# Block-sparse attention and an MLP on one core: half of the masks moved off TensorE, Softplus from its table throughout, other buffers for streamed weights, and a new order on all engines

## The chip, the core and the metric

The kernel runs on one core of a Trainium2 chip. A core has engines with queues of their own: TensorE (PE in the profile), VectorE (DVE), ScalarE (ACT), GpSimd (POOL) and SyncE (SP), which here issues the DMAs. Each works through its own instructions in order and waits on semaphores for the others. The metric is the device time of one execution in microseconds. Lower is better.

## The reference

All arrays are f32.

```
# attention: B=4, H=8, S=768, D=64; blocks of 32 keys, window 16
k_sum = k in blocks of 32, max;   v_sum = v in blocks of 32, mean
local  = q k^T / 8      where |i - j| < 16, else -1e9
far    = q k_sum^T / 8 + log(32)
a      = softmax over [local, far]
attn   = a [v, v_sum]                                    # 4, 8, 768, 64
# MLP on x = attn as 3072 tokens x 512
h = x w_in                                               # w_in 512 x 2048
g = h * erf(softplus(h))
out = g w_out                                            # w_out 2048 x 512
```

## The kernel before, in words

**Tokens and stages.** The 3072 tokens are cut into 6 columns of 512. Attention goes by quads: a quad is one column and one pair of heads, 24 in all (NQ). For a quad, `scores` multiplies queries by a window of 96 keys and 24 block sums (L565) into two PSUM banks pA and pB, and `softmax` follows: maxima on DVE (`red`, L596 or L600), a negation and scaling (L610, L615), exponentials on ACT (L606), reciprocal (L618) and normalisation (L622, or L625 on ACT). Then transposes (L636), a copy to SBUF (L641), the product with the values (L662), and the split of x into a high part `xh` and a low part `xl` (L678, from the fifth column part on L706 to L719).

**Masks.** For the first MQ = 8 quads the window's mask is added by TensorE: `mask` issues an L556 and an L557 for each of the two banks before the scores are accumulated on top, and `red` then reads the two banks with two L600. For the other quads DVE adds the mask (`add`, two L591, from PSUM to SBUF), and one L596 takes the maxima.

**The MLP** goes by 24 chunks k: a token column and a quarter of the 2048 hidden columns. For k < 8, `mm1` (L765) multiplies x by w_in, in three products of high and low parts; `hout` copies the result from PSUM. For k >= FAST = 8, `products` (L806) takes a form with seven products, for which weight sums are prepared by `add_up` (L394, L397, L403, L406), written to DRAM and fetched again by `get_sums` (L433). The activation comes next. For k < SOFT = 4 it is Tanh (L781) and a Ln (L879), for the other chunks Softplus from its table (L783, L872), then Erf (L884) in both. `gsplit` multiplies by h (L896; L891 for k < 2) and splits the product into `gh` (a cast, L277) and `gl` (a subtraction, L903). `mm2` multiplies these by w_out (L920; L916 for k < 2 in plain f32).

**Weights.** `load_w` brings a 1 MB unit of w_in or w_out as 64-bit numbers. `convert` makes f32 of it on DVE (L330, L333, L336), and `split` makes a high half on ACT (`high`, a cast, L277) and a low half on DVE (`low`, L352). Conversions of 16 units stand among the first four chunks. Units of w_in stay in SBUF. The halves of w_out are written to DRAM by `put` (L366) and come back by `get` (L376, `w<-dr` in the profile) from chunk 7 on into five slots which `turn` hands out in the order of ROUND. `get_sums` takes slots from the same round. Slot 11 is also the buffer `sums` of `add_up`, whose last reader is the L406 of the last set of sums.

**Order.** Nothing is issued as it stands in the loop. `on`, `act`, `pe` and `dma` record every step in a `Plan` with its cost on each engine that may run it; `order` then lists the steps, each engine taking what is ready and has the smallest key (due time plus the step's entry in TUNE; an entry can also pin an engine). Where a step names two engines, the one that would end it first gets it. The issued program has a fixed order on each engine. FILL puts small matmuls on a tile of zeros (`busy`, L959) ahead of certain TensorE steps in the first part.

Of the kernel before, what the change touches and what calls it, by code (L numbers as in the profile page):

```python
# [23 lines left out]
NP = H // 2  # L24
# [10 lines left out]
NG = F // (128 * G)  # L35
NPER = NCH * NG
MQ = 2 * NP
# [4 lines left out]
SOFT = 4  # L42
FAST = 8
# [3 lines left out]
FILL = {20: 7, 40: 8, 41: 9, 61: 6, 93: 14, 111: 6}  # L47
# [3 lines left out]
def f32(ap):  # L51
    return ap.bitcast(F32)
# [134 lines left out]
def block_attention_mlp(ctx: ExitStack, tc: tile.TileContext, q_t, k_nat, k_win, v_tok, v_nat, v_win, w_in, w_out, out):  # L187
# [8 lines left out]
    def sb(shape, dtype, name, tag=None):  # L196

        n = math.prod(shape[1:])
        if n % 128 == 0:
            return pool.tile(shape, dtype, name=name, tag=tag or name)  # L200
        t = pool.tile([128, -(-n // 128) * 128], dtype, name=name, tag=tag or name)[0:shape[0], 0:n]
        return t if len(shape) == 2 else t.rearrange("p (a b) -> p a b", a=shape[1]) if len(shape) == 3 else t.rearrange("p (a b c) -> p a b c", a=shape[1], b=shape[2])
# [47 lines left out]
    def stat(n, par):  # L250
        return stats[:, (3 * par + n) * NB:(3 * par + n + 1) * NB]
# [12 lines left out]
    def pe(us, fn, r=(), w=(), **kw):  # L264
        return P.add({"PE": us}, lambda e: fn(), r, w, **kw)

    def on(us, fn, r=(), w=(), **kw):
        return P.add(us, lambda e: fn(engines[e]), r, w, **kw)

    def act(us, fn, r=(), w=(), **kw):  # L270
        return P.add({"ACT": us}, lambda e: fn(), r, w, **kw)
# [4 lines left out]
    def copy(e, o, i):  # L276
        e.copy(o, i) if e is nc.scalar else e.tensor_copy(o, i)  # L277

    units = [(kind, g, r) for kind, g in UNITS for r in range(2)]
    tiles, raws, whl, w32, wide = {}, {}, {}, {}, {}
    WHOLE = {0: 11, 1: 10}
    FIRST = {4: 9, 5: 8, 6: 12, 7: 13}
    LATER = {0: 12, 1: 13, 2: 9, 3: 8, 4: 9, 5: 8}
    ROUND = (12, 13, 11, 9, 8)
    ON_DVE = (0, 2)
    SUMS, TURN, RAW_X = 11, (12, 13), 10  # L290
    kept = {}

    def slot(n, shape, dtype, name):
        return sb(shape, dtype, name, f"w{n}")

    def number(u):
        return 2 * u[1] + u[2]

    def raw_slot(u):
        return number(u) if u[0] == "i" else 12 + u[2]  # L300

    def frees(n):
# [12 lines left out]

    def convert(u):

        w, s, m = f"w{raw_slot(u)}", {}, number(u)
        at_once = u[0] == "i" or u[1] >= NN
        home = f"gl{u[2]}" if at_once else f"a{m}"  # L320

        def a():
            if at_once:
                s["t"] = sb([128, 2, 512], F32, "a32", home)
            else:
                if u[2] == 0:
                    wide[u[1]] = slot(WHOLE[u[1]], [128, 2, 2, 512], F32, "a32s")
                s["t"] = w32[u] = wide[u[1]][:, u[2]]
            s["a"], s["rw"] = s["t"].bitcast(U32), raws.pop(u)
            nc.vector.tensor_scalar(s["a"], s["rw"][..., 1], 3, 0x3FFFFFFF, op0=ALU.logical_shift_left, op1=ALU.bitwise_and)  # L330

        def b():
            nc.vector.scalar_tensor_tensor(s["a"], s["rw"][..., 0], 29, s["a"], op0=ALU.logical_shift_right, op1=ALU.bitwise_or)  # L333

        def c():
            nc.vector.scalar_tensor_tensor(s["a"], s["rw"][..., 1], 0xC0000000, s["a"], op0=ALU.bitwise_and, op1=ALU.bitwise_or)  # L336

        on({"DVE": 0.6}, lambda e: a(), [w], [home] if at_once or u[2] else frees(WHOLE[u[1]]))
        on({"DVE": 1.13}, lambda e: b(), [w, home], [home])
        on({"DVE": 1.13}, lambda e: c(), [w, home], [home])  # L340
        if at_once:
            split(u, m if u[0] == "i" else FIRST[m], home, lambda: s["t"])

    def split(u, n, home, whole):
        def high(e):
            t = slot(n, [128, 2, 2, 512], F32R, "w")
            whl[u] = t[:, 0], t[:, 1]
            kept[u] = t
            copy(e, whl[u][0], whole())

        def low(e):
            e.tensor_tensor(whl[u][1], whole(), f32(whl[u][0]), op=ALU.subtract)  # L352
        on({"ACT": 0.94}, high, [home], frees(n))
        on({"DVE": 1.13}, low, [home, f"w{n}"], [f"w{n}"])

    def parts(m, n):
        u = ("o", m // 2, m % 2)
        split(u, n, f"a{m}", lambda: w32[u])
# [65 lines left out]
    def turn():  # L424
        turns[0] += 1
        return ROUND[(turns[0] - 1) % len(ROUND)]

# [117 lines left out]
    def scores(qd, banks=PA):  # L545
# [3 lines left out]
        def mask():  # L549
# [3 lines left out]
            m0 = mask_at[qd // NP % 3]  # L553
            for sc in s["sc"] if qd < MQ else []:

# [3 lines left out]
        def keys(parts):  # L559
            for j in range(NB):  # L560
                for a in range(2):
                    r, o = slice(64 * a, 64 * a + 64), slice(64 * (j % 2), 64 * (j % 2) + 64)
                    for n, rhs in parts(r, j):
                        n += j // 2 * NK
                        nc.tensor.matmul(s["sc"][a][o, n:n + rhs.shape[-1]], lhsT=s["qb"][r, 64 * j:64 * j + 64], rhs=rhs, start=qd >= MQ, stop=True, skip_group_check=True)  # L565

# [8 lines left out]
        if qd >= NP:  # L575
            pe(1.06 if qd >= MQ else 1.64, both, ["qb", "kw"] + (["mh"] if qd < MQ else []), banks)
        else:
# [4 lines left out]
    def softmax(qd, banks=PA):  # L582
# [10 lines left out]
        def red(e):  # L593
            s["mx"] = stat(0, par)
            if qd >= MQ:
                e.tensor_reduce(s["mx"], s["pr"], op=ALU.max, axis=AX.X)  # L596
# [5 lines left out]
        def exps():  # L602
            sm = s["sm"] = stat(1, par)
            for j in range(NB):
                i = j % NI
                nc.scalar.activation(s["pr"][:, j], s["pr"][:, j] if qd >= MQ else s["sc"][j // NI][:, i * NK:(i + 1) * NK], AF.Exp, scale=0.125, bias=s["mx"][:, j:j + 1], accum_out=sm[:, j:j + 1])  # L606

# [3 lines left out]

        if qd >= MQ:
            on({"DVE": 1.2}, add, banks, [pr])
# [156 lines left out]
    def hout(k, f, eng):  # L770
# [7 lines left out]
        def tanh():  # L778
            wt[k, s] = sb([128, 2, T], F32, "wt", f"wt{s}")
            if k < SOFT:  # L780
                nc.scalar.activation(wt[k, s], hc[k, s], AF.Tanh, scale=0.5)  # L781
# [6 lines left out]
    def soft(k, s, fn):  # L788
        act(0.96 if k < SOFT else 1.06, fn, [f"hc{s}"], [f"wt{s}"], table=("sig", "exp") if k < SOFT else ("soft",))

# [84 lines left out]
    def logs(k):  # L875

        for n in range(2 if k < SOFT else 0):
            s = f"wt{n}"
            act(1.06, lambda n=n: nc.scalar.activation(wt[k, n], wt[k, n], AF.Ln, scale=-0.49999994, bias=half_b), [s], [s], table=("log",))  # L879

    def erfs(k, after):
        for n in range(2):
            s = f"wt{n}"
            act(0.96, lambda n=n: nc.scalar.activation(wt[k, n], wt[k, n], AF.Erf, scale=-1.0 if k < SOFT else 1.0), [s], [s], table=("sig",), after=after)  # L884

# [135 lines left out]
    def follow(n, bank=None):  # L1021
        sums(n, bank)
        load_quad(n)
        with_quad(load_nat, n + 1)

    with_quad(load_nat, NP)
    for u in units[4:6]:
        load_w(u)

    todo = {0: units[2:6], 1: units[6:10], 2: units[10:14], 3: units[14:16]}  # L1030
    loads = {0: units[6:12], 1: units[12:14], 2: units[14:16]}
    early = FAST
    early_att = {(1, 1): [(lambda n: follow(n, "o2"), 4)], (1, 3): [(attend, 4), (follow, 5)],
                 (2, 1): [(output, 4), (attend, 5), (follow, 6)], (2, 3): [(output, 5), (attend, 6), (follow, 7)],
                 (3, 1): [(output, 6), (attend, 7), (follow, 8)], (3, 3): [(output, 7), (attend, 8), (follow, 9)]}

    for k in range(NPER):
        qa, qs = k + NP, k + NP + 1
        ch, g = divmod(k, NG)
        mult = sub = {"DVE": 1.136}  # L1040
        cast = {"DVE": 0.605, "ACT": 0.95} if NG <= k < FAST else {"DVE": 0.605}
        xeng, heng = ({"DVE": 0.6, "ACT": 0.48},) * 2 if k < early else ({"DVE": 0.6},) * 2
        for u in todo.get(k, []):
            convert(u)
        for u in loads.get(k, []):
            load_w(u)
        if k == 3:
            for m in (4, 5, 6, 7):
                put(m, FIRST[m])
        if k == 4:  # L1050
            for m in (2, 3):
                parts(m, LATER[m])
            for c in range(2):
# [95 lines left out]
    k = NPER - 1  # L1149
# [59 lines left out]
```

## Time and profile before

| | before |
|---|---|
| median of 3 runs | 629.37 us (629.01 to 630.21) |
| profiled execution | 629.01 us, span 627.2 us |
| granted clock of TensorE, mean | 0.997 |
| busy: PE, DVE, ACT, POOL | 618.2, 440.3, 409.6, 46.4 us |

The span runs from the first to the last instruction; 1.8 us of the time lie around it. The profiled execution is the fastest of the three, 0.36 us under the median. A busy time counts an engine's instructions from start to end, and neighbours overlap by some hundredths of a microsecond, so a pitch is a little less than a mean duration. In the views below, "a<-b" stands for the output and inputs by the program's names, "x4" for a count, and the engine behind "<-" ended the wait that is named.

### The profile page before, as it was taken

How to read it: one execution, taken by the hardware profiler on the slowest of the kernel's cores; microseconds unless marked ns; L12 is line 12 of the kernel's file. 1: busy time of each engine (PE TensorE's matmuls, PEld its weight loads, DVE VectorE, ACT ScalarE, POOL GpSimd, SP SyncE). 2: the span in 40 equal slices, each digit the busy share in tenths (PEclk: the TensorE clock that was granted, in tenths of full speed). 3: DMA queues.
4: the chain of work that ended last, by engine and by line, in shares of the span. 5: the costliest groups of instructions: out<-in, count | busy, mean ns of one | idle time of the engine just before them, and what ended most of it. 6: DMA issues, size and time to landing. Idle time of an engine off the chain costs nothing.

```text
span 627.2 us, 12062 instructions
## 1 busy us (share of the span) xinstructions
PE 618.2 (99%) x4840; PEld 520.9 (83%) x4840; DVE 440.3 (70%) x634; ACT 409.6 (65%) x820; POOL 46.4 (7%) x72
## 2 busy tenths in 40 slices
PE   9999999999999997999999999999999999999997
PEld 6786567888888886889899899898898898899886
DVE  5999999848799797768668657658656576425442
ACT  5669977979969677464585675565766555552550
POOL 2010000100420800000000000000000000000000
PEclk9999999999999999999999999999999999999999
DMA  8998957653585888888767776766687555574622
GB/s 327 274 364 300 330 162 254 242 193 87 186 326 178 313 286 327 286 315 285 277 222 248 267 275 215 249 222 227 221 291 253 195 181 195 202 258 157 253 72 67
DMA packets 36843, 150.23 MB, mean 240 GB/s; under 512 B 3956, under 2 KB 9396, under 8 KB 24244
## 3 DMA queue, kind: packets, MB, share of 16 engines
q1 hardware_dynamic: 36212, 148.95, 68.4%
q8 instruction: 38, 0.62, 0.4%
q10 hardware_dynamic: 576, 0.52, 0.3%
q14 instruction: 17, 0.14, 0.1%
HBM read 124.13 MB, written 23.07 MB: 235 GB/s over the span
## 4 chain that ended last, share of the span: by engine, by line
PE 91%; DVE 5%; DMA 1%; ACT 1%; issue 1%; SPq 0%; DVEq 0%
PE ops L920 37%; PE hb L806 14%; PE h L765 13%; PE ha L806 10%; PE ops L916 4%; PE px L662 4%; PE pA L565 3%; PE pA L636 2%; PE pB L636 1%; DMA w<-dr 1%; PE idle L959 1%; ACT prf L606 1%; DVE ws L406 1%; DVE gl L903 1%; DVE sums L397 0%
## 5 line engine op out<-in xcount | busy, mean ns | idle before, releaser
L920 PE MATMUL ops<-w,gh 128*128 128x512 f32 x704 | 230.1, 396 | 2.7 <-DMA w<-dr 2.7
L920 PEld LDWEIGHTS ops<-w,gh 128*128 128x128 f32 x704 | 133.0, 189 | 30.5 <-DMA w<-dr 2.9
L920 PE MATMUL ops<-w,gl 128*128 128x512 f32 x352 | 137.8, 391 | 0.0
L896 DVE TENSOR_TENSOR hc<-wt,hc 128x1024 f32<-128x1024 f32 x44 | 54.7, 1253 | 77.3 <-ACT wt L884 77.3
L1167 ACT ACT_TABLE_LOAD x83 | 106.5, 1283 | 1.5
L765 PE MATMUL h<-xh,w 128*128 128x512 f32 x256 | 86.9, 403 | 0.1
L277 ACT COPY hc<-hb 128x256 f32<-128x256 f32 x49 | 18.1, 373 | 95.4 <-DVE hc L859 40.4
L920 PEld LDWEIGHTS ops<-w,gl 128*128 128x128 f32 x352 | 66.5, 189 | 12.4
L765 PEld LDWEIGHTS h<-xh,w 128*128 128x128 f32 x256 | 48.1, 188 | 12.1 <-issue 1.1
L806 PE MATMUL hb<-w,ws 128*128 128x256 f32 x384 | 56.8, 283 | 0.0
L903 DVE TENSOR_TENSOR gl<-hc,gh 128x1024 fp32r<-128x1024 f32 x44 | 54.8, 1246 | 0.8
L606 ACT ACTIVATE pr<-pr,stats 128x120 f32<-128x120 f32 x128 | 48.8, 382 | 5.8 <-DVE stats L615 5.7
L806 PEld LDWEIGHTS hb<-w,ws 128*128 128x128 f32 x384 | 50.7, 192 | 0.2 <-DVE ws L406 0.2
L884 ACT ACTIVATE wt<-wt 128x1024 f32<-128x1024 f32 x48 | 50.6, 1062 | 0.4
L765 PE MATMUL h<-xl,w 128*128 128x512 f32 x128 | 49.9, 390 | 0.0
L527 POOL COPY kw<-ksum 128x96 f32<-128x96 f32 (+1 forms) x28 | 17.3, 632 | 405.6 <-DMA kw<-k_win 367.6
L277 DVE CAST gh<-hc 128x1024 fp32r<-128x1024 f32 x43 | 30.0, 698 | 18.1 <-PE ops L920 16.9
L872 ACT ACTIVATE wt<-hc 128x1024 f32<-128x1024 f32 x32 | 32.1, 1050 | 0.2
L277 DVE COPY hc<-hb 128x256 f32<-128x256 f32 x47 | 19.8, 422 | 15.2 <-PE hb L806 13.9
L916 PE MATMUL ops<-a32s,gw 128*128 128x512 f32 x64 | 29.3, 596 | 0.0
L806 PE MATMUL ha<-w,ws 128*128 128x256 f32 x192 | 28.5, 283 | 0.8 <-DVE w L743 0.8
L856 DVE TENSOR_TENSOR hc<-hb,hc 128x256 f32<-128x256 f32 x32 | 13.5, 422 | 22.3 <-PE hb L806 20.7
(168 smaller groups left out, 1110.7 us busy)
## 6 DMA issues: line engine op xcount, KB each, us to landing
w<-dr SPq DMA_DIRECT2D x36, 1024.0 KB
ws<-ds SPq DMA_DIRECT2D x30, 1024.0 KB
kw<-k_win SPq DMA_DIRECT2D x20, 480.0 KB
rw<-w_in SPq DMA_DIRECT2D x8, 1024.0 KB
rw<-w_out SPq DMA_DIRECT2D x8, 1024.0 KB
dr<-w SPq DMA_DIRECT2D x8, 1024.0 KB
ds<-ws SPq DMA_DIRECT2D x8, 1024.0 KB
vw<-v_win SPq DMA_DIRECT2D x20, 384.0 KB
```

The lines of the kernel that those rows point to most:

```text
L277: e.copy(o, i) if e is nc.scalar else e.tensor_copy(o, i)
L606: nc.scalar.activation(s["pr"][:, j], s["pr"][:, j] if qd >= MQ else s["sc"][j // NI][:, i * NK:(i + 1) * NK], AF.Exp, scale=0.125, bias=s ...
L662: nc.tensor.matmul(xo[r, o], lhsT=s["vw"][:, j, r], rhs=s["pt"][:, a, o], start=True, stop=True)
L765: nc.tensor.matmul(hs[k, f][:, 0:T], lhsT=w[m], rhs=xt[ch, cc][x], start=(cc == 0 and n == 0), stop=(cc == 3 and n == 2))
L806: nc.tensor.matmul(shape, lhsT=w[m], rhs=y[l], start=first and c == 0 and i == 0, stop=c == 1 and i == 2, skip_group_check=True)
L872: nc.scalar.activation(wt[k, n], hc[k, n], AF.Softplus)
L884: act(0.96, lambda n=n: nc.scalar.activation(wt[k, n], wt[k, n], AF.Erf, scale=-1.0 if k < SOFT else 1.0), [s], [s], table=("sig",), after ...
L896: e.tensor_tensor(hc[k, n], wt.pop((k, n)), hc[k, n], op=ALU.mult)
L903: e.tensor_tensor(gs[k, n][1], hc.pop((k, n)), f32(gs[k, n][0]), op=ALU.subtract)
L916: nc.tensor.matmul(os_[ch, t], lhsT=x[0][:, i % 2, t * 128:(t + 1) * 128], rhs=w32["o", g, i // 2][:, i % 2], start=first, stop=last)
L920: nc.tensor.matmul(os_[ch, t], lhsT=x[y][:, i % 2, t * 128:(t + 1) * 128], rhs=w[m], start=first and n == 0, stop=last and n == 2)
L1167: nc.scalar.preload_act_table_set(sets[o["load"]])
```

## The change

- MQ goes from 8 to 4: quads 4 to 7 get their mask from DVE as the later ones do.
- SOFT goes from 4 to 0: Softplus from its table (L783) in all chunks; Tanh and Ln go, and Erf no longer has a scale of -1.
- ROUND goes from (12, 13, 11, 9, 8) to (12, 13, 9, 8, 11).
- `low` of `split` may also run on POOL, at a planner cost of 2.9 against 1.13 on DVE; `high` of `gsplit` may run on ACT in all of the first eight chunks.
- TUNE has 2071 entries instead of 464, and other values; FILL has 30 matmuls in four places instead of 50 in six. So the order on every engine is another one.

```diff
-MQ = 2 * NP
+MQ = NP
...
-SOFT = 4
+SOFT = 0
...
-TUNE = {0: (-833.887, 1.5, 0, None), 1: (-504.34, 1.5, 0, None), ...}
-FILL = {20: 7, 40: 8, 41: 9, 61: 6, 93: 14, 111: 6}
+TUNE = {0: (-1842.48, 1.5, 0, None), ...}
+FILL = {48: 4, 51: 6, 81: 10, 86: 10}
...
-    ROUND = (12, 13, 11, 9, 8)
+    ROUND = (12, 13, 9, 8, 11)
...
         on({"ACT": 0.94}, high, [home], frees(n))
-        on({"DVE": 1.13}, low, [home, f"w{n}"], [f"w{n}"])
+        on({"DVE": 1.13, "POOL": 2.9}, low, [home, f"w{n}"], [f"w{n}"])
...
-        cast = {"DVE": 0.605, "ACT": 0.95} if NG <= k < FAST else {"DVE": 0.605}
+        cast = {"DVE": 0.605, "ACT": 0.95} if k < FAST else {"DVE": 0.605}
```

In counts of instructions: L556 and L557 on PE 16 to 8 each, L959 64 to 44; L352 on DVE 16 to 6 and on POOL 0 to 10; L591 on DVE 32 to 40, L596 16 to 20, L600 16 to 8; on ACT L781 and L879 8 to 0 each, L783 8 to 16, L625 8 to 0 with L622 on DVE 23 to 24, casts of 1024 columns 17 to 22 (on DVE 43 to 38), table loads 83 to 86 ahead of L1167.

The first place is POOL's queue from the constants to the sums. A kw copy (L527) puts block sums into a tile of keys. Before:

```order
L507 COPY vwf<-vsum 24x1024
L527 COPY kw<-ksum 128x4x24 x8
L527 COPY kw<-ksum 128x8x24 x3
L394 TENSOR_TENSOR sums<-w 128x2x256 x4
L397 TENSOR_TENSOR sums<-sums 128x2x256 x3
```

After, at the same place (a_512 and the like are the f32 units that `convert` made):

```order
L507 COPY vwf<-vsum 24x1024
L352 TENSOR_TENSOR w<-a_512,w 128x1024
L352 TENSOR_TENSOR w<-a_573,w 128x1024
L527 COPY kw<-ksum 128x4x24 x4
L352 TENSOR_TENSOR w<-a_785,w 128x1024
L352 TENSOR_TENSOR w<-a_817,w 128x1024
L352 TENSOR_TENSOR w<-a_890,w 128x1024
L527 COPY kw<-ksum 128x4x24
L352 TENSOR_TENSOR w<-a_910,w 128x1024
L527 COPY kw<-ksum 128x4x24
L352 TENSOR_TENSOR w<-a_1017,w 128x1024
L527 COPY kw<-ksum 128x4x24
```

Low halves stand between the copies now, and the copies behind them wait their turn; three more follow after these rows.

The second place is DVE's queue up to the first `gl` (L903), which the first L920 needs. Before:

```order
L277 CAST gh<-hc 128x1024
L330 TENSOR_SCALAR a_1111<-rw 128x1024
L333 SCALAR_TENSOR_TENSOR a_1111<-rw,a_1111 128x1024
L352 TENSOR_TENSOR w<-a_1073,w 128x1024
L336 SCALAR_TENSOR_TENSOR a_1111<-rw,a_1111 128x1024
L678 TENSOR_TENSOR xl<-px,xh 128x512
L600 TENSOR_REDUCE stats<-pA 128x4
L600 TENSOR_REDUCE stats<-pB 128x4
L352 TENSOR_TENSOR w<-a_1111,w 128x1024
L615 TENSOR_SCALAR stats<-stats 128x8
L330 TENSOR_SCALAR a_1197<-rw 128x1024
L903 TENSOR_TENSOR gl<-hc,gh 128x1024
```

After:

```order
L330 TENSOR_SCALAR a_1115<-rw 128x1024
L333 SCALAR_TENSOR_TENSOR a_1115<-rw,a_1115 128x1024
L610 TENSOR_SCALAR stats<-stats 128x8
L336 SCALAR_TENSOR_TENSOR a_1115<-rw,a_1115 128x1024
L618 RECIPROCAL stats<-stats 128x8
L622 TENSOR_TENSOR pr<-pr,stats 128x960
L277 CAST xh<-px 128x512
L678 TENSOR_TENSOR xl<-px,xh 128x512
L352 TENSOR_TENSOR w<-a_1115,w 128x1024
L330 TENSOR_SCALAR a_1190<-rw 128x1024
L903 TENSOR_TENSOR gl<-hc,gh 128x1024
```

From the start of the program to this first L903, DVE has 3 L352 instead of 11. It has 6 L591, 3 L596 and 2 L600 instead of 8 L600, two more L622, one L610 and one L618 more, one cast of `gh` fewer, and one cast of `xh` and one copy of `hc` more.

The third place is SP's queue around chunk 8, where the halves of w_out (dr4 to dr7) are fetched for chunks 6 and 7. Numbers are those of tiles: w_2530 and w_2339 are the tiles for dr6. Before:

```order
L376 DMA w_2190<-dr4_1182 128x2048
L410 DMA ds20_2209<-ws_2088 128x2048
L410 DMA ds21_2237<-ws_2110 128x2048
L376 DMA w_2263<-dr5_1253 128x2048
...
L376 DMA w_2422<-dr7_1398 128x2048
L536 DMA vw_2449<-v_win 96x1024
L518 DMA qb_2469<-q_t 128x512
L433 DMA ws_2482<-ds10_2007 128x2048
L540 DMA vw_2449<-vsum_109 24x8x128
L410 DMA ds00_2504<-ws_2432 128x2048
L376 DMA w_2530<-dr6_1297 128x2048
```

After:

```order
L376 DMA w_2169<-dr4_1202 128x2048
L536 DMA vw_2192<-v_win 96x1024
L518 DMA qb_2207<-q_t 128x512
L376 DMA w_2223<-dr5_1276 128x2048
L540 DMA vw_2192<-vsum_109 24x8x128
L410 DMA ds31_2246<-ws_2190 128x2048
L410 DMA ds30_2271<-ws_2197 128x2048
L376 DMA w_2339<-dr6_1326 128x2048
L410 DMA ds01_2364<-ws_2298 128x2048
L536 DMA vw_2401<-v_win 96x1024
L518 DMA qb_2427<-q_t 128x512
L376 DMA w_2434<-dr7_1367 128x2048
```

The tile for dr6 now comes ahead of that for dr7, ahead of the sums' last writes (L410 of ds0) and ahead of the first fetch of sums (L433); by ROUND it lies in slot 9, where w_2169 was, and no longer in slot 11.

2 lines of the change are left out of this document (1 added, 1 removed).

## The prediction

> **What bounds the kernel now.** I read first the page's busy time and its chain.
>
> ```profile
> PE 618.2 (99%) x4840; PEld 520.9 (83%) x4840; DVE 440.3 (70%) x634; ACT 409.6 (65%) x820; POOL 46.4 (7%) x72
> ...
> PE 91%; DVE 5%; DMA 1%; ACT 1%; issue 1%; SPq 0%; DVEq 0%
> ```
>
> TensorE (PE) is busy 618.2 of 627.2 us. A gain is therefore PE work taken away or one of its few waits taken away; a loss is a new wait. The list of PE's waits names the waits:
>
> ```profile
> PE ops L920 <- DMA w<-dr: 2.7, 1, 2.7
> PE idle L959 <- DVE zeros L212: 1.1, 1, 1.1
> PE ha L806 <- DVE w L743: 0.8, 1, 0.8
> ```
>
> The table by stages shows how near VectorE (DVE) is to being the bound in the first sixth (columns: length, then busy time of PE, PEld, DVE, ACT, POOL, PE's granted clock, DMA share and rate):
>
> ```profile
> 40.00:60.00 20.00, 20.00 (x125) 13.22 (x122) 19.61 (x24) 17.20 (x33) 0.95 (x2) 1.00 0.90 334
> 60.00:80.00 20.00, 20.00 (x102) 12.28 (x101) 19.93 (x23) 19.82 (x25) 0.00 (x0) 1.00 0.89 320
> 80.00:100.00 20.00, 20.00 (x99) 12.48 (x98) 19.33 (x23) 14.29 (x29) 1.56 (x2) 1.00 0.49 143
> ...
> 120.00:140.00 20.00, 20.00 (x147) 16.40 (x148) 9.84 (x16) 15.97 (x30) 0.69 (x2) 1.00 0.66 223
> ...
> 200.00:250.00 50.00, 46.25 (x298) 39.22 (x297) 41.92 (x56) 37.41 (x70) 15.08 (x9) 0.99 0.86 300
> ```
>
> From 40 to 100 us DVE is busy 58.9 of 60 us, and PE never waits: the two run abreast. After 120 us DVE has half its time free. The meeting point is the first `gl` (L903), which the first L920 matmul needs:
>
> ```profile
> 106.94 1.22 DVE L903 TENSOR_TENSOR gl<-hc,gh 128x1024 fp32r<-128x1024 f32 x1
> ...
> 110.47 0.16 DVE L610 TENSOR_SCALAR stats<-stats 128x8 f32<-128x8 f32 x1
> ...
> 108.54 0.39 PE L765 MATMUL h<-xh,w 128*128 128x512 f32 x1
> 108.76 0.39 PE L920 MATMUL ops<-w,gh 128*128 128x512 f32 x1
> ```
>
> DVE ends it at 108.16, and PE is there at 108.76: 0.6 us of slack. The other weak place is chunk 8, where the 200 to 250 us row has PE idle for 3.75 us. The chain of waits there:
>
> ```profile
> 237.67 1.15 DVE ws L406
> ...
> 238.87 8.58 DMA w<-dr
> ...
> 247.50 4.30 PE ops L920 x12
> ```
>
> The w_out half of get(6) comes into slot 11, the buffer of the sums, which the last L406 frees at 238.82; then it needs 8.58 us. The wait is followed by a half clock:
>
> ```profile
> 249.00:252.40 3.40, 3.40 (x11) 2.69 (x10) 1.23 (x1) 1.86 (x2) 0.00 (x0) 0.50 0.53 193
> ```
>
> 3.4 us at 0.50 cost 1.7 us.
>
> **The change, part by part.** All against the profiled run, 629.0 us (span 627.2 and 1.8 around it); it is the fastest of three, and the median is 0.4 above.
>
> Mask. PE's part of it for one quad, four matmuls ahead of the scores:
>
> ```profile
> 102.31 0.37 PE L556 MATMUL pA<-mask_h,small 128*128 128x480 bf16 x1
> ...
> 102.89 0.31 PE L565 MATMUL pA<-kw,qb 64*64 64x120 f32 x1
> ```
>
> 102.31 to 102.89 is 0.58 us. Four quads lose it: -2.3 us of PE work, all of it after the point where DVE binds, because the order puts as much other PE work ahead of the first L920 as it takes away. On DVE each such quad gets two L591 and an L596 for two L600; three of the four stand ahead of the first `gl` and are counted below, the fourth lies in DVE's free half after 120 us.
>
> ROUND. get(6) now goes to slot 9, get(7) to slot 8, and neither waits for the sums. The 3.75 us idle in that row (2.7 and 0.8 of them listed) and the 1.7 us of half clock go: -5.5 us. What is late next is get(6) itself: between the last reader of slot 9 and its first L920 stand some 6.3 us of PE work (24 matmuls of 512 columns at 0.22 to 0.23 us, the pitch of the PE rows at 108.54 and 108.76, and about 0.9 us of small ones). A landing of 8.58 us would leave 2.3 us of wait, one faster than 6.3 us none. I take none and keep 2.3 for the range.
>
> Softplus, casts and table loads, on ScalarE (ACT). In four chunks L783 takes the place of L781 and L879 goes; eight L625 go; up to five L277 casts and three table loads come:
>
> ```profile
> L1167 ACT ACT_TABLE_LOAD x83 | 106.5, 1283 | 1.5
> ...
> L277 ACT CAST w<-a 128x1024 fp32r<-128x1024 f32 x12 | 12.6, 1052 | 4.6 <-DVE a L336 4.6
> ...
> L879 ACT ACTIVATE wt<-wt,stats 128x1024 f32<-128x1024 f32 x8 | 9.3, 1160 | 0.1
> ...
> L625 ACT ACTIVATE prf<-prf,stats 128x120 f32<-128x120 f32 x8 | 2.4, 384 | 0.0
> ```
>
> -9.3 - 2.4 + 5 x 1.05 + 3 x 1.28 = -2.6 us of ACT, beside PE's work: costed at nothing. ACT is full only in the 60 to 80 us row (19.82 of 20). Were a cast put just there, the DVE operation behind it would come up to 1.05 us later; at the first `gl`, where ACT has had 14.29 of 20 us just before, that is covered.
>
> Fillers. 20 fewer L959. At the start PE waits for DVE's conversions anyway, so what goes as filler partly returns as wait:
>
> ```profile
> L959 PE MATMUL idle<-zeros 128*128 128x256 bf16 x64 | 9.7, 305 | 1.1 <-DVE zeros L212 1.1
> ```
>
> By its busy time 20 of 64 are 3.0 us: 0 to -3.0, taken -0.8, nearer to none since DVE is ahead of PE by only 0.6 us at the place where they end up. It counts only if PE, and not DVE, sets the time at the first `gl`.
>
> L352. Eight of the ten that go to GpSimd (POOL) leave DVE ahead of the first `gl`. The rows for what leaves and comes there (line, shapes, count, busy, mean ns):
>
> ```profile
> L352 DVE TENSOR_TENSOR w<-a,w 128x1024 fp32r<-128x1024 f32 x12 | 14.6, 1220 | 0.5 <-ACT w L277 0.5
> ...
> L596 DVE TENSOR_REDUCE stats<-pr 128x8 f32<-128x960 f32 x16 | 18.3, 1143 | 0.0
> ...
> L591 DVE TENSOR_TENSOR pr<-pA,mask_sb 128x480 f32<-128x480 f32 x16 | 10.4, 652 | 7.4 <-PE pB L565 7.4
> ...
> L600 DVE TENSOR_REDUCE stats<-pA 128x4 f32<-128x480 f32 x5 | 3.3, 655 | 1.1 <-PE pB L565 1.1
> ...
> L622 DVE TENSOR_TENSOR prf<-prf,stats 128x960 f32<-128x960 f32 x3 | 3.5, 1150 | 0.0
> ```
>
> Rows overlap by 0.08 us, so the pitch is that much less. By pitch: -8 x 1.14 (L352), +3 x 1.06 (L596), L591 for L600 even (6 x 0.57 each), +2 x 1.07 (L622, a quad's normalisation that now stands earlier), two 512-wide copies and casts for one 1024-wide (+0.6), 0.3 of small operations: -2.9 us. Uncontended, the first `gl` would end at 108.16 - 2.9 = 105.3, with PE there at about 108.0: 2.7 us of slack.
>
> But POOL isn't free of DVE. The one place of this trace where POOL does such work on full tiles, and DVE beside it:
>
> ```profile
> 202.71 7.33 POOL L394 TENSOR_TENSOR sums<-w 128x512 f32<-128x512 f32 x4 [2.97 <-DVE ws L406]
> 210.01 7.24 POOL L397 TENSOR_TENSOR sums<-sums 128x512 f32<-128x512 f32 x4
> ```
>
> ```profile
> 202.49 1.22 DVE L896 TENSOR_TENSOR hc<-wt,hc 128x1024 f32<-128x1024 f32 x1
> 203.62 2.32 DVE L903 TENSOR_TENSOR gl<-hc,gh 128x1024 fp32r<-128x1024 f32 x1
> 205.86 0.94 DVE L452 TENSOR_REDUCE vs_sum<-rows 128x24 f32<-128x768 f32 x1
> ...
> 207.88 1.01 DVE L277 CAST gh<-hc 128x1024 fp32r<-128x1024 f32 x1 [0.23 <-PE ops L920]
> 208.82 1.25 DVE L610 TENSOR_SCALAR stats<-stats 128x8 f32<-128x8 f32 x1
> ...
> 211.35 2.02 DVE L622 TENSOR_TENSOR pr<-pr,stats 128x960 f32<-128x960 f32 x1
> ```
>
> ```profile
> 175.47 1.29 POOL L397 TENSOR_TENSOR sums<-sums 128x512 f32<-128x512 f32 x1
> ```
>
> Alone a POOL operation on 512 columns takes 1.29 us; here 1.83. Beside it the L903 takes 2.32 instead of 1.22, and the L610, a few columns, 1.25 instead of the 0.16 at 110.47, while the reduce L452 keeps its 0.94. That is not a shared rate: one waits until the other's whole instruction is over, and operations that read one tile to a few numbers, or read PSUM, are spared. An L352 on POOL is twice as long, 2 x 1.29 = 2.6 us. From below: from 203.6 to 213.4 DVE lost 3.4 us (1.1 in L903, 0.3 in the cast, 1.1 in L610, 0.9 in L622 against its 1.15) to 5.3 POOL operations, 6.8 us of POOL's own work: 0.5 us for each us of POOL, 1.3 for an L352. From above: every L352 blocks one for nearly its length, 2.3. I take 1.8, the middle, because most DVE work in that stage (conversions, L891, L903) is of the kind that blocks, and a reduce of 0.94 no longer covers 2.6. 8 x 1.8 = 14.4: the first `gl` ends at 119.7 instead of 108.16, and PE, 0.1 later, starts at 119.8 instead of 108.76: +11.0 us. Queued behind it on PE is everything after, and DVE has room only later. After such a wait I count one half-clock period, +1.7.
>
> [...]
>
> Sum: 629.0 + 11.0 + 1.7 - 2.3 - 5.5 = 633.9, say 634.
>
> **Rivals.**
> 1. POOL's part hides, DVE isn't held: no wait at the first `gl`. 629.0 - 2.3 - 5.5 - 0.8 = 620.4. For it: the conversions leave DVE 2.9 us less nominal work. Against: the 2.32 us row. It decides at a loss of 2.7 / 8 = 0.34 us for each L352; below that this is the case. It is the one that ends faster.
> 2. DVE is held, but at the low end, 1.3: the first `gl` at 115.7, +7.0, and 629.0 + 7.0 + 1.7 - 2.3 - 5.5 = 629.9; without the half clock 628.2. No difference to be measured, or little.
> 3. DVE is held to the full, 2.3: the first `gl` at 123.7, +15.0: 637.9, and with the late get(6) (2.3, and 1.7 for another half clock) 641.9.
> 4. ROUND doesn't do what it says: get(6) waits as long as before in its new place. With rival 1, 620.4 + 4.0 = 624.4; with the forecast 638.
> Loss at the other weak point, POOL's queue: an L352 that stands behind a kw copy (L527) waiting for its load comes late for PE. The copies' load wait isn't in PE's list now, and this adds to case 3 rather than making one.
>
> **How the numbers follow.** Forecast (held, 1.5 to 2.1 us each, 631 to 636): 0.4. Rival 3 with the late get(6) and rival 4 on the forecast: 0.2. Rival 2: 0.13, half of it (0.07) within 0.2% (1.3 us, about what a measurement of this kernel can tell from no change), 0.02 faster, 0.04 slower. Rival 1, with rival 4 or not: 0.27. Faster 0.29, same 0.07, slower 0.64. The range must reach rival 1 at 620, since it holds more than 2 in 10, and up to the full hold: 619.5 to 641. The forecast alone: 631 to 636.
>
> **What would show it.** In the profile after: POOL's L352 with a mean over 2.6 us; DVE's conversions (L333, L336) beside them at 2 to 3.5 us instead of 1.22; in PE's list waits for `gl` or `gw` (L903, L891) or `w` of some 11 us before 130 us, with a clock of 0.5 behind; no wait of L920 on the load around chunk 8 over 2.3 us; four L556 pairs fewer. If PE waits for DVE under 1 us in all and the span is near 619, rival 1 held. If the mean of L333 and L336 stays at 1.22 and PE is still late, my mechanism is wrong whatever the time.

## The result, and the profile after

The changed kernel takes 636.81 us (median of four runs, 635.39 to 638.65) against 629.19 before: 1.0128 times as long, with a 95% interval of 1.0089 to 1.0167. The forecast was 634 with a range of 619.5 to 641, on the slow side. The profiled execution is the slowest of the four, 638.65 us with a span of 636.9, 9.7 more than before.

Busy times and chain of the page, after:

```profile
PE 618.1 (97%) x4804; PEld 517.6 (81%) x4804; DVE 442.0 (69%) x621; ACT 411.2 (65%) x815; POOL 82.4 (13%) x82
...
PE 81%; DVE 11%; ACT 3%; DMA 2%; issue 1%; SPq 1%; ACTq 0%
```

PE's busy time is 0.1 us from that of before, with less work in it: slices at half clock are a part of what makes it longer (two stretches of 3.4 us at 0.50, at 27 and at 98 us, where before had one). The span grew, so the loss is waiting. PE's waits, after:

```profile
PE ops L916 <- DVE gw L891: 3.1, 2, 1.7
PE ops L916 <- DVE a32s L336: 3.1, 1, 3.1
PE h L565 <- issue: 1.6, 1, 1.6
PE pA L636 <- DVE pr L622: 1.3, 1, 1.3
PE px L662 <- DMA vwf<-v_win: 1.3, 1, 1.3
PE h L765 <- DVE hc L277: 1.3, 1, 1.3
```

The wait on `w<-dr` is gone, and most of what has come ends at DVE. The stages (same columns as in the prediction):

```profile
14.00:40.00 26.00, 23.13 (x320) 17.71 (x320) 21.75 (x32) 15.43 (x58) 3.50 (x2) 0.93 1.01 268
40.00:60.00 20.00, 17.14 (x120) 11.92 (x120) 19.25 (x19) 13.32 (x15) 5.23 (x4) 1.00 0.74 273
60.00:80.00 20.00, 18.32 (x90) 10.61 (x89) 19.83 (x21) 17.28 (x33) 6.35 (x4) 1.00 0.95 324
80.00:100.00 20.00, 16.92 (x85) 10.44 (x84) 20.00 (x22) 12.82 (x28) 9.41 (x5) 0.96 0.49 159
...
200.00:250.00 50.00, 48.69 (x333) 39.30 (x332) 45.56 (x60) 38.70 (x57) 14.53 (x9) 1.00 0.66 236
```

Where PE lost nothing from 40 to 100 us before, it is now idle 7.6 of 60 us, with DVE busy 59.1. At 200 to 250 it is idle 1.3 instead of 3.75. The meeting point, on DVE and on PE:

```profile
122.07 1.22 DVE L903 TENSOR_TENSOR gl<-hc,gh 128x1024 fp32r<-128x1024 f32 x1
```

```profile
123.50 0.39 PE L920 MATMUL ops<-w,gh 128*128 128x512 f32 x1
```

The first L920 starts at 123.50 instead of 108.76, 14.7 later; from there to the end it is 513.4 instead of 518.4 us, 5.0 less.

### The profile page after: what moved, and what is told of

It is laid out like the page before. It is cut to its first block, busy times and chain, and to the rows that moved or that the text cites. A ratio compares the mean times of both kernels' runs of the same rounds, so it can differ in the third digit from the quotient of the medians.

```text
span 636.9 us, 11998 instructions
## 1 busy us (share of the span) xinstructions
PE 618.1 (97%) x4804; PEld 517.6 (81%) x4804; DVE 442.0 (69%) x621; ACT 411.2 (65%) x815; POOL 82.4 (13%) x82
## 4 chain that ended last, share of the span: by engine, by line
PE 81%; DVE 11%; ACT 3%; DMA 2%; issue 1%; SPq 1%; ACTq 0%
PE ops L920 38%; PE hb L806 14%; PE ha L806 11%; PE h L765 8%; PE px L662 3%; DMA vwf<-v_win 2%; PE pA L565 2%; DVE a L333 2%; DVE a L336 2%; PE pA L636 2%; PE pB L636 2%; ACT L1167 1%; DVE a L330 1%; DVE pr L622 1%; DVE hc L896 1%
## 5 line engine op out<-in xcount | busy, mean ns | idle before, releaser
L920 PE MATMUL ops<-w,gh 128*128 128x512 f32 x704 | 233.7, 396 | 0.0
L920 PEld LDWEIGHTS ops<-w,gh 128*128 128x128 f32 x704 | 132.5, 188 | 28.4 <-issue 0.9
L920 PE MATMUL ops<-w,gl 128*128 128x512 f32 x352 | 137.4, 390 | 0.0
L765 PE MATMUL h<-xh,w 128*128 128x512 f32 x256 | 91.2, 410 | 2.3 <-DVE hc L277 1.3
L920 PEld LDWEIGHTS ops<-w,gl 128*128 128x128 f32 x352 | 66.3, 188 | 12.0
L606 ACT ACTIVATE pr<-pr,stats 128x120 f32<-128x120 f32 x160 | 61.0, 382 | 8.1 <-DVE stats L615 7.9
L527 POOL COPY kw<-ksum 128x96 f32<-128x96 f32 (+1 forms) x28 | 24.0, 868 | 313.1 <-DMA kw<-k_win 297.0
L765 PEld LDWEIGHTS h<-xh,w 128*128 128x128 f32 x256 | 48.1, 188 | 15.8 <-issue 2.3
L903 DVE TENSOR_TENSOR gl<-hc,gh 128x1024 fp32r<-128x1024 f32 x44 | 56.3, 1282 | 0.8
L765 PE MATMUL h<-xl,w 128*128 128x512 f32 x128 | 50.1, 391 | 0.5 <-DVE xl L678 0.5
L277 DVE CAST gh<-hc 128x1024 fp32r<-128x1024 f32 x38 | 27.1, 713 | 15.6 <-PE ops L920 14.4
L916 PE MATMUL ops<-a32s,gw 128*128 128x512 f32 x64 | 30.7, 611 | 6.2 <-DVE gw L891 3.1
L606 ACT ACTIVATION_READ_ACCUMULATOR pr<-pr,stats 128x1 f32 x160 | 29.9, 187 | 0.0
L765 PEld LDWEIGHTS h<-xl,w 128*128 128x128 f32 x128 | 24.1, 188 | 7.0 <-issue 1.9
```

The lines of the kernel that those rows point to most:

```text
L765: nc.tensor.matmul(hs[k, f][:, 0:T], lhsT=w[m], rhs=xt[ch, cc][x], start=(cc == 0 and n == 0), stop=(cc == 3 and n == 2))
L903: e.tensor_tensor(gs[k, n][1], hc.pop((k, n)), f32(gs[k, n][0]), op=ALU.subtract)
L916: nc.tensor.matmul(os_[ch, t], lhsT=x[0][:, i % 2, t * 128:(t + 1) * 128], rhs=w32["o", g, i // 2][:, i % 2], start=first, stop=last)
L920: nc.tensor.matmul(os_[ch, t], lhsT=x[y][:, i % 2, t * 128:(t + 1) * 128], rhs=w[m], start=first and n == 0, stop=last and n == 2)
```

## The experiments

Ratios are to runs of the kernel before taken beside each kernel (their medians lie between 627.8 and 629.2), with 95% intervals. "First L920" is its start in the profiled execution.

| kernel | median us | ratio | first L920 | span |
|---|---|---|---|---|
| before | 629.2 | 1 | 108.8 | 627.2 |
| changed | 636.8 | 1.0128 (1.0089 to 1.0167) | 123.5 | 636.9 |
| e1, changed, L352 on DVE | 630.6 | 1.0026 (1.0008 to 1.0044) | 114.0 | 627.3 |
| e2, changed, POOL's L352 a memset | 623.7 | 0.9934 (0.9909 to 0.9959) | 108.5 | 621.9 |
| e3, before, L352 on POOL | 633.0 | 1.0083 (1.0054 to 1.0112) | 115.1 | 631.2 |
| e4, before, new ROUND | 625.1 | 0.9947 (0.9927 to 0.9967) | 108.4 | 622.2 |
| e5, changed again | 635.4 | 1.0124 (1.0099 to 1.0148) | 121.2 | 634.6 |
| e6, before, masks, new plan | 643.0 | 1.0254 (1.0220 to 1.0289) | 117.3 | 639.3 |
| e7, before, Softplus, new plan | 631.0 | 1.0063 (1.0039 to 1.0086) | 113.0 | 631.5 |
| e8, changed, POOL's L352 in quarters | 629.9 | 1.0029 (1.0015 to 1.0043) | 115.4 | 629.1 |
| e9, before, masks, order kept | 631.5 | 1.0052 (1.0026 to 1.0079) | 109.5 | 627.7 |
| e10, before, Softplus, order kept | 630.5 | 1.0051 (1.0030 to 1.0072) | 111.6 | 627.9 |
| e11, before, ROUND and quarters | 626.9 | 0.9984 (0.9967 to 1.0001) | 109.6 | 623.4 |
| e12, e11 with fewer fillers | 627.0 | 0.9981 (0.9963 to 1.0000) | 111.0 | 624.8 |

**Is it GpSimd that holds VectorE?** First the changed kernel with the low halves back on DVE.

```diff
+        if "low" in o:
+            o["on"] = "DVE"
         o["fn"](o["on"])
```

> The changed kernel with all ten L352 of GpSimd back on VectorE, at the same places of the order. Theory (GpSimd's L352 hold VectorE): VectorE loses the 13 us of stretched operations before the first gl and gets 8 x 1.14 = 9.1 us of work back, so the first L920 comes 3 to 4 us earlier than its 123.5, about 633 us. Rival (the L352 on GpSimd are hidden and the order alone is late): VectorE gets 9 us more and loses none, 645 us. L333 and L336 return to a mean of 1.22 to 1.28 us under the theory.

630.6 us, 6 less than the changed kernel. DVE has 9.1 us more to do ahead of the first L920 and reaches it 9.5 us earlier than in the first trace (7.2 earlier than in e5's), more than the 3 to 4 expected. The stretches at half clock are gone, too: the mean clock is 1.000. PE still waits 3.5 us for L891 and L336 there, against 6.2 in the changed kernel, so a part of these waits belongs to the rest of the change. DVE's groups with what stretched, first of the changed kernel from 14 to 130 us, then of e1 from 14 to 123 us:

```profile
L333 DVE SCALAR_TENSOR_TENSOR a<-rw,a 128x1024 uint32<-128x1024 uint32 x12 | 18.9, 1578 | 0.1
L336 DVE SCALAR_TENSOR_TENSOR a<-rw,a 128x1024 uint32<-128x1024 uint32 x12 | 16.3, 1362 | 0.1
...
L891 DVE TENSOR_TENSOR gw<-wt,hc 128x1024 f32<-128x1024 f32 x4 | 7.0, 1758 | 0.6 <-ACT wt L884 0.6
L336 DVE SCALAR_TENSOR_TENSOR a32s<-rw,a32s 128x1024 uint32<-128x1024 uint32 x4 | 6.9, 1732 | 0.0
L622 DVE TENSOR_TENSOR pr<-pr,stats 128x960 f32<-128x960 f32 x3 | 5.5, 1825 | 0.0
...
L596 DVE TENSOR_REDUCE stats<-pr 128x8 f32<-128x960 f32 x4 | 4.6, 1148 | 0.0
```

```profile
L336 DVE SCALAR_TENSOR_TENSOR a<-rw,a 128x1024 uint32<-128x1024 uint32 x12 | 14.6, 1218 | 0.1
L333 DVE SCALAR_TENSOR_TENSOR a<-rw,a 128x1024 uint32<-128x1024 uint32 x12 | 14.6, 1218 | 0.1
...
L336 DVE SCALAR_TENSOR_TENSOR a32s<-rw,a32s 128x1024 uint32<-128x1024 uint32 x4 | 4.9, 1224 | 0.0
...
L891 DVE TENSOR_TENSOR gw<-wt,hc 128x1024 f32<-128x1024 f32 x4 | 4.9, 1220 | 0.6 <-ACT wt L884 0.6
...
L622 DVE TENSOR_TENSOR pr<-pr,stats 128x960 f32<-128x960 f32 x3 | 3.5, 1153 | 0.0
```

Count times the difference of the means: 4.3 + 1.7 + 2.2 + 2.0 + 2.0 = 12.2 us in these groups. The reduce L596 did not stretch (1.148 us, 1.144 in e1), but none of the four lies beside an L352 on POOL. Others do: from 74.88 to 81.63 us POOL has two L352, and beside them the reduce L452 keeps its 0.94 us (0.943 in e1) and the two L591, which read PSUM and SBUF, their 0.64 (0.648 and 0.646), where the L891 takes 3.36 instead of 1.22:

```profile
76.06 3.36 DVE L891 TENSOR_TENSOR gw<-wt,hc 128x1024 f32<-128x1024 f32 x1
79.33 0.94 DVE L452 TENSOR_REDUCE vs_sum<-rows 128x24 f32<-128x768 f32 x1
80.20 0.64 DVE L591 TENSOR_TENSOR pr<-pA,mask_sb 128x480 f32<-128x480 f32 x1
80.76 0.64 DVE L591 TENSOR_TENSOR pr<-pB,mask_sb 128x480 f32<-128x480 f32 x1
```

All of DVE's operations together are its busy time ahead of the first `gl`, in the changed kernel, in its second trace (e5) and in e1 (length, busy time and count, then PE's clock, DMA share and rate):

```profile
0.00:122.07 122.07, 107.24 (x125) 0.97 0.79 259
0.00:119.75 119.75, 108.09 (x125) 0.99 0.78 264
0.00:112.55 112.55, 102.19 (x133) 1.00 0.83 278
```

Without its eight L352 (9.1 us) e1 would have 93.1. So DVE lost 14.1 and 15.0 us, 1.8 to 1.9 for each of the eight L352. Not only operations with two inputs in SBUF were held: L330 reads one tile, takes 0.69 us in the mean in e1, and once, in e5, beside an L352 on POOL from 34.21 to 36.60 us, took 2.90:

```profile
34.24 2.90 DVE L330 TENSOR_SCALAR a<-rw 128x1024 uint32<-128x1024 uint32 x1
```

One case by itself, on POOL and on DVE, from the timelines of the changed kernel:

```profile
37.87 2.49 POOL L352 TENSOR_TENSOR w<-a,w 128x1024 fp32r<-128x1024 f32 x1 [18.97 <-ACT w L277]
```

```profile
38.15 3.30 DVE L333 SCALAR_TENSOR_TENSOR a<-rw,a 128x1024 uint32<-128x1024 uint32 x1
```

L352 ends at 40.36; the L333 ends at 41.45, 1.1 later, about its own length (1.22 in e1). The next pair repeats it: an L352 from 44.60 to 47.00 us, and an L333 of 3.41 from 44.68, which ends 1.1 behind it. By these two rows it moved when the other was over. The next experiment leaves the engine and the time and takes the reading away.

```diff
-            e.tensor_tensor(whl[u][1], whole(), f32(whl[u][0]), op=ALU.subtract)
+            e.memset(f32(whl[u][1]), 0.0) if e is nc.gpsimd else e.tensor_tensor(...)
```

> The changed kernel, but the ten low halves that GpSimd makes are filled with zeros by a memset of the same 128x1024 tile, which reads nothing (the low parts of those weights are left out). Theory (VectorE is held while GpSimd reads two tiles of SBUF): L333, L336, L891, L622 return to 1.15 to 1.3 us, the first L920 comes 9 to 12 us earlier, 625 us, with one or two half-clock periods fewer. Rival (GpSimd holds VectorE by writing too): still some 1 us for each, 631. Rival (the order or the loads at the start are late whatever GpSimd does): 636.

623.7 us. POOL's L352, and DVE's L333 beside it:

```profile
L352 POOL MEMSET w<- 128x1024 f32 x10 | 9.5, 960 | 35.2 <-DVE a L336 28.3 <-issue 6.9
```

```profile
L333 DVE SCALAR_TENSOR_TENSOR a<-rw,a 128x1024 uint32<-128x1024 uint32 x12 | 14.7, 1223 | 0.1
```

Beside GpSimd's memset, which only writes SBUF, L333 loses nothing measurable (1.223 us, 1.218 in e1), and the first L920 is back at 108.5 us. DVE's busy time ahead of the first `gl`, for the same 125 instructions as in the changed kernel, is 13.2 us less than in its first trace and 14.0 less than in e5:

```profile
0.00:106.63 106.63, 94.06 (x125) 1.00 0.85 288
```

(The memset is also shorter, 0.96 us, and doesn't wait for the cast: what is shown by it alone is that the order isn't late of itself once DVE has this room.) With the subtraction on GpSimd the mean of L333 is 1.58 us, with the memset 1.22. Whether the missing read or the shorter instruction does it, this run alone doesn't show; the quarters of e8 below, shorter still at 0.72 to 0.75 us, read SBUF and bring L333 to 1.31.

Then the reverse, in the kernel before.

```diff
+        if o.get("low") in (('i', 0, 1), ('i', 1, 0), ..., ('o', 0, 0)):   # the same ten units
+            o["on"] = "POOL"
         o["fn"](o["on"])
```

> The kernel before with the same ten L352 (by weight unit) on GpSimd, at their places in its own order, nothing else changed. Theory: 8 of them ahead of the first gl cost VectorE 1.65 us each and free it of 1.14 each, +4 us, and the next conversions wait for the slower low halves: 633 to 637 us. Rival (GpSimd's part is hidden): VectorE gets 9 us of room, 628 to 629 us.

633.0 us, with the first L920 at 115.1, 6.4 later than before. Of this, 2.1 us lie ahead of the first L765 (31.22 instead of 29.14): PE waited 2.0 us for a load of q at 7.95 us, ahead of any L352, and ran at half clock for 3.4 us after it. The 4.3 behind the first L765 are the theory's 4. So this part alone, in an order that had nothing to do with it, costs 0.83% (0.54 to 1.12). All three runs lie at or within 2.5 us of the theory's numbers, and not at the rivals' 645, 631 and 628.

**Does the length of one hold matter?**

```diff
+            for c, h in ((0, 0), (0, 1), (1, 0), (1, 1)) if e is nc.gpsimd else ():
+                i = slice(256 * h, 256 * h + 256)
+                e.tensor_tensor(whl[u][1][:, c, i], whole()[:, c, i], f32(whl[u][0])[:, c, i], op=ALU.subtract)
+            if e is nc.gpsimd:
+                return
```

> The changed kernel with each L352 of GpSimd cut into four of 256 columns. Theory (VectorE is held for the length of one GpSimd instruction, and operations that are spared cover a part): a hold of 0.65 us is covered more often, the loss per low half falls from 1.65 towards 1.3 us, 8 x 0.35 = 2.8 us, 634 us. Rival (what counts is GpSimd's total reading time): 636 to 637 us, as whole. Rival (each piece waits for VectorE anew, and low halves come later): over 638 us.

629.9 us, 4 us better than expected. The groups on POOL (L354 is the subtraction in this kernel) and on DVE from 14 to 123 us:

```profile
L354 POOL TENSOR_TENSOR w<-a,w 128x256 fp32r<-128x256 f32 x32 | 38.3, 1227 | 36.3 <-ACT w L277 36.3
```

```profile
L333 DVE SCALAR_TENSOR_TENSOR a<-rw,a 128x1024 uint32<-128x1024 uint32 x12 | 15.7, 1312 | 0.1
```

DVE's busy time ahead of the first `gl` in this kernel:

```profile
0.00:114.53 114.53, 99.91 (x125) 1.00 0.83 274
```

A quarter takes 1.23 us in the mean, and 0.72 to 0.75 in half of the 40 cases: now POOL waits, too. DVE loses 0.09 us on an L333 instead of 0.36, and over all its operations 5.9 us against e2 (6.8 against e1 without its L352) instead of 13.2 to 15.0. Expected were 1.3 us for each low half; it is 0.7 to 0.9. The same columns are read in both kernels; what differs is the length of one instruction, at least 2.39 us for an L352 in the changed kernel's first trace. It still isn't better than L352 on DVE (e1, 1.0026 against 1.0029): DVE waited 2.4 us for loads and 1.9 us for POOL's halves.

**The start.** The first profile begins badly, so the changed kernel was profiled once more, unchanged.

> The changed kernel once more, for a second trace of its start. In its first profile the first L765 starts at 31.15 us after a late v_win load and two half-clock slices; with the same order up to there it starts at 27.3 and 28.0 in the two runs with GpSimd's L352 taken away. Theory (the late start of the first profile is a matter of that execution's loads): first L765 at 27 to 29 us, the waits of the stage with L352 as before, 635 to 637 us. Rival (GpSimd's work is what makes the start late): again 31 us.

635.4 us, and the first L765 starts at 27.5. In the first profile these slices are the difference:

```profile
27.00:28.00 1.00, 1.00 (x7) 0.50 1.27 228
28.00:29.00 1.00, 1.00 (x6) 0.50 0.86 227
29.00:30.00 1.00, 1.00 (x6) 0.50 1.04 325
```

They follow the 1.6 us wait of L565 and the late v_win load in the list above, of which e5 has 0.8 and 0.3 us. So about 2 us of the first trace's 14.7 belong to that execution and not to the change; in e5 the first L920 stands at 121.2, 12.4 us later than before, with its waits on L891 and L336 at 3.1 and 3.0 as in the first.

**ROUND alone.**

```diff
-    ROUND = (12, 13, 11, 9, 8)
+    ROUND = (12, 13, 9, 8, 11)
```

> The kernel before with the new ROUND alone. Theory: get(6) no longer waits for the sums; the wait of 2.7 us, the 0.8 of L743 as far as it hangs on it, and 1.7 us of half clock go: 624 to 626 us. Rival (the wait only moves, or get(6) is as late in slot 9): 629.

625.1 us. PE's waits in this kernel, all of them:

```profile
PE idle L959 <- DVE zeros L212: 1.1, 1, 1.1
PE hb L806 <- ACT hc L277: 0.9, 1, 0.9
PE o L565 <- issue: 0.6, 1, 0.6
PE pA L636 <- DVE pr L622: 0.4, 1, 0.4
```

The wait on `w<-dr` and the half clock behind it are gone, the span is 5.0 us shorter than in the profile of before, and a wait of 0.9 us stands in their place. The medians differ by less, 3.3 us (2.1 to 4.6); e9 below shows a reason. It is the fastest kernel of this study that computes everything, 0.53% (0.33 to 0.73) faster than before.

**Masks alone.** The first try changed the cost and the dependences that the planner sees, too.

```diff
-            for sc in s["sc"] if qd < MQ else []:
+            for sc in s["sc"] if qd < NP else []:
...
+            if NP <= qd < MQ:
+                add(e)
+                e.tensor_reduce(s["mx"], s["pr"], op=ALU.max, axis=AX.X)
+                return
...
-        on({"DVE": 1.06 if qd >= MQ else 1.14}, red, ..., [f"mx{par}"])
+        on({"DVE": ... 2.26}, red, ..., [f"mx{par}"] + ([pr] if NP <= qd < MQ else []))
```

> The kernel before with the masks of quads 4 to 7 on VectorE alone (two additions and one reduce over both banks in place of two reduces; same places in the order). Theory (VectorE is the bound up to the first gl): three of the quads lie ahead of it and add 1.06 us each, so the first L920 comes some 2.5 us later, and 0.6 of mask goes behind: 630 to 631.5 us. Rival (TensorE is the bound, VectorE has room): 2.3 us faster, 626.5.

643.0 us, far outside both. PE's waits:

```profile
PE h L769 <- DVE xl L682: 4.3, 2, 2.3
PE h L769 <- DVE xh L277: 2.0, 1, 2.0
PE h L769 <- ACT hc L277: 2.0, 1, 2.0
```

(L769 is L765 of the kernel before.) These are waits of mm1 on x and on emptied banks, not on masks, and PE ran at half clock for 10.2 us at and behind some of them: the planner, given another cost, had laid everything out anew with numbers found for the old plan. This run says nothing of the masks. The second try gives the planner the old costs and changes only what is issued.

```diff
-            for sc in s["sc"] if qd < MQ else []:
+            for sc in s["sc"] if qd < NP else []:
...
+            if NP <= qd < MQ:
+                add(e)
-            if qd >= MQ:
+            if qd >= NP:
                 e.tensor_reduce(s["mx"], s["pr"], op=ALU.max, axis=AX.X)
```

> The kernel before with the masks of quads 4 to 7 on VectorE, every instruction else at the place it has before (in the last try the planner had made another order). Theory (VectorE is the bound up to the first gl): three quads ahead of it at 1.06 us, less 0.6 of slack and 0.6 of mask behind: 630 to 631.5 us. Rival (TensorE is the bound): 626.5. Rival (the masks on VectorE cost as much as in the last try): 640.

631.5 us, 0.52% (0.26 to 0.79) slower, as the theory of DVE as the bound has it. The profiled execution shows only a part: it is the fastest of its ten runs, and its first L920 is 0.7 us later. It also shows that the half clock does not follow the wait at chunk 8 in each execution. The wait is as long as before (L922 is L920 here), and the 5 us from its end on are at full clock (before, the half clock began 1.5 us behind the end of the wait):

```profile
PE ops L922 <- DMA w<-dr: 2.8, 1, 2.8
```

```profile
249.60:254.60 5.00, 4.97 (x26) 4.19 (x27) 1.23 (x1) 4.80 (x7) 0.00 (x0) 1.00 0.70 257
```

**Softplus alone.** Again with the planner's new order first, then with the order kept.

```diff
-            if k < SOFT:
+            if False:
                 nc.scalar.activation(wt[k, s], hc[k, s], AF.Tanh, scale=0.5)
...
-    act(1.06, lambda n=n: nc.scalar.activation(..., AF.Ln, ...), [s], [s], table=("log",))
+    act(0.0, lambda: None, [s], [s])
```

> The kernel before with Softplus from its table in the first four chunks in place of Tanh and Ln (the places of the Ln stay in the order, empty). Theory (ScalarE's work lies beside TensorE's): no change, 628.5 to 629.5 us. Rival (ScalarE, full from 60 to 80 us, is what VectorE's L891 wait for there): up to 2 us faster.

631.0 us, slower than either expectation. For the order of before, the planner keeps the old entries, and loads are set as the operations are issued:

```diff
-        if "load" in o:
-            nc.scalar.preload_act_table_set(sets[o["load"]])
+        need = o.get("real", o["table"])       # ("soft",) for L783, () for the empty Ln
+        if o["on"] == "ACT" and need and now not in need:
+            now = need[-1]
+            nc.scalar.preload_act_table_set(sets[now])
```

> The kernel before with Softplus from its table in the first four chunks, in the order of before, without the Ln, table loads where they are needed. Theory (ScalarE's work is hidden): 628 to 629.5 us. Rival (Softplus itself costs time in that stage, as the last try with another order seemed to say): 631.

630.5 us: the rival's number. ACT's timeline, before and then in e10, at the first activation, whose input was there at 44.69 and at 45.41:

```profile
44.73 1.06 ACT L781 ACTIVATE wt<-hc 128x1024 f32<-128x1024 f32 x1
```

```profile
45.43 1.28 ACT L1169 ACT_TABLE_LOAD   x1
46.72 1.06 ACT L783 ACTIVATE wt<-hc 128x1024 f32<-128x1024 f32 x1
```

Tanh found its table loaded; Softplus needs one just there. PE's list in e10 has three new waits of 0.9 us, each on ACT:

```profile
PE px L662 <- ACT prf L625: 0.9, 1, 0.9
PE h L765 <- ACT vsum L461: 0.9, 1, 0.9
PE h L765 <- ACT hc L277: 0.9, 1, 0.9
```

The first, on L625, comes ahead of any Softplus and can be this execution's own; the other two stand behind table loads and amount to 1.8 us. The trace of e7 has waits at the same two places, of 0.9 and 1.8 us, and not the first. ACT's busy time fell in e10, from 409.6 to 403.0 us. By these rows the work was hidden and the place of the loads was not; no run moves the loads alone. How much of the changed kernel's time comes from this wasn't separated, since its order is another.

**Towards a faster version.** e11 joins the edits of e3, e4 and e8 (ten low halves on GpSimd, in quarters, and the new ROUND, in the order of before); e12 has 20 fillers fewer besides.

```diff
-FILL = {20: 7, 40: 8, 41: 9, 61: 6, 93: 14, 111: 6}
+FILL = {20: 7, 40: 8, 41: 9, 61: 6}
```

> The kernel before with the new ROUND, and ten L352 on GpSimd in quarters of 256 columns, at their places in its own order. Theory (a short hold hardly delays VectorE, GpSimd waits instead; VectorE has room, and TensorE with its fillers is the bound): first L920 at 108 us as before, 624.5 to 625.5 us, as with ROUND alone. Rival (late low halves hold the next conversion): 627 to 629 us.

626.9 us. Between the theory and the rival, and not better than ROUND alone (0.9984, up to 1.0001, against 0.9947): PE waited 1.5 us for L622.

> The same without the last two groups of fillers (20 of 50). Theory: VectorE's room lets TensorE use what the fillers took, 2 us: 623 us. Rival (the time of the fillers comes back as waits): 625, or with a half-clock period 626.5.

627.0 us. The rival held: what the fillers left came back as waits, 2.9 us from 14 to 40 us.

## Why the prediction was right, and where it wasn't

**L352 and the first gl: right.** Forecast 1.8 us for each low half, 14.4 in all; measured 13.2 and 14.0 against e2, 14.1 and 15.0 against e1. The nominal work was right as well: with the eight L352 back on DVE the forecast's 105.3 for the end of the first `gl` becomes 114.4, and e1 ends it at 113.8. Forecast for the first L920 119.8 us, measured 123.5 and 121.2, with the half clock that the sum counted apart (+1.7) inside: in both traces it lies ahead of the first L920, behind the wait on L336 (3.1 and 3.0 us), and not behind a wait for the `gl`. As the prediction said of the signs to look for, L333 came to 3.3 us beside an L352, the eight L352 on POOL to a mean of 2.86, and the waits fell on L891 and conversions. They came in pieces of up to 3.1 us, though, and not as one of 11, and the `gl` itself was not waited for: PE was late by then through `gw` and `a32s`. That operations which read PSUM were spared, as the forecast has it, is in the trace of before too, where two L591 keep the 0.65 us of their mean beside POOL:

```profile
171.15 0.65 DVE L591 TENSOR_TENSOR pr<-pA,mask_sb 128x480 f32<-128x480 f32 x1
171.71 0.65 DVE L591 TENSOR_TENSOR pr<-pB,mask_sb 128x480 f32<-128x480 f32 x1
```

```profile
171.19 4.04 POOL L397 TENSOR_TENSOR sums<-sums 128x512 f32<-128x512 f32 x3
```

**Fillers and start: not steady.** -0.8 was taken, in rival 1's sum alone. e2 is near rival 1, since DVE isn't held in it (L333 at 1.22 us): its first L920 comes 0.2 us earlier than before, and it takes 623.7 us where rival 1 has 620.4. The first L765 came 1.6 us earlier than before in e5 (27.5 against 29.14) and 2.0 later in the first trace (31.15). As the prediction has it, an earlier start counts only where PE sets the time at the first `gl`; that a late load can make the start late for DVE too was not foreseen.

**Chunk 8: right in mechanism, too large.** -5.5 for the wait and the clock; ROUND alone gave 5.0 of span against the one profile of before, and 3.3 by the medians. The 1.7 us of half clock in the term belong to some executions only: before has them behind its 2.7 us, e9 has none behind 2.8. In the changed kernel 1.3 us came back as a new wait, which the forecast did not have:

```profile
228.59 0.50 PE L765 MATMUL h<-xh,w 128*128 128x512 f32 x1 [1.29 <-DVE hc L277]
```

It stands in e1 and e2 too. The rival on get(6) (up to 2.3 us) did not happen.

**Masks: the mis-sized term.** -2.3 "all of it after the point where DVE binds". Behind the first L920 the span shrank by 5.0 in all, of which waits and clock are 3.75 + 1.7 - 1.3 = 4.15. That leaves 0.9 us of less work, not 2.3. The work itself went as forecast: behind the first L920 the changed kernel lacks four mask matmuls, and eight L636 and three L765 that now stand ahead of it, in place of the masks of three quads. By the starts of PE's rows that is 2.1 us less than in e4. But the 704 L920 on `gh` take 1.9 us more, at full clock in both. Behind the first L920 PE goes over from L920 to other matmuls 75 times in the changed kernel and 54 times in e4, and at some of these changes an L920 takes 0.3 us to the next start, instead of 0.23, as here (the L565 starts 0.32 after the first, and the next L920 0.34 after the last):

```profile
125.32 0.39 PE L920 MATMUL ops<-w,gh 128*128 128x512 f32 x1
125.64 0.31 PE L565 MATMUL pA<-kw,qb 64*64 64x120 f32 x1
...
126.62 0.50 PE L920 MATMUL ops<-w,gh 128*128 128x512 f32 x1
```

60 of the 704 take over 0.3 us in the changed kernel and 44 in e4. So the new order gave back by its changes most of what the masks' matmuls had taken; this is read from the traces, and no run tests it. e9 shows that masks on DVE don't pay in the order of before.

**Softplus: wrong.** Costed at nothing; alone in the old order it costs 0.51% (0.30 to 0.72), 3.2 us. Less work for ACT did not mean no later results: the table loads, 1.28 us each, came where PE waits for ACT (two waits of 0.9 us).

So the sum, 4.9 us of loss, came to 7.4 in e5 (12.4 ahead of the first L920, 5.0 back behind it) and 9.7 in the first profile. In e5 the front agrees within 0.3 us, 12.4 against 11.0 + 1.7, and that is in part luck: the `gl` ends at 121.0, 1.3 later than forecast, since DVE also sat idle 1.3 us longer than in e1, and whether the half clock cost anything isn't shown, since PE waited for DVE again behind it (1.4 us for L622). The miss of the sum lies behind it, in the masks' 2.3 and the new 1.3.

## What to carry to other kernels

Before work is moved from VectorE to GpSimd, look for the rows where both already run on SBUF: a VectorE duration that grows by about the length of the GpSimd instruction (here an L333 from 1.22 to 3.30 us beside an L352 of 2.49) says that the move can give back more than it takes (here 13 to 15 us for 9.1), however idle GpSimd looks. If it must be moved, try it cut into shorter instructions: here quarters (1.23 us in the mean and 0.72 to 0.75 in half of the cases, where a whole one took 2.39 and more) more than halved the loss, though leaving the work on VectorE was as fast. When an order is planned from costs, test a part of a change by keeping the issued order and altering only the instruction; a plan made anew for one changed cost and dependence lost 11.5 us here (e6 against e9) which the part itself did not.

## What was not expected of the hardware

Cutting one GpSimd instruction in four took more than half of the loss from VectorE, 5.9 to 6.8 us instead of 13.2 to 15.0, and made GpSimd wait: a quarter took 1.23 us in the mean and 0.72 to 0.75 in half of the cases. The length of one wait on PE did not tell whether the clock would halve: 2.7 us were followed by 3.4 us at half clock before, and 2.8 us at the same place in e9 were not; two waits of 1.3 and 1.6 us near one another were, in the first profile of the changed kernel.
